# Six edits and three smaller ones at once in a tuned training step: later gradient transposes, the time reorder on VectorE, earlier down weights, k copied in parts, a shared layer norm, three blocks at once in the down product; more buffers for two tiles, a later pump

## The chip, the cores and the metric

One core of one Trainium2 chip. The metric is the device time of one execution in microseconds (us), the median of several executions. One execution is also profiled. Two of all executions were in a slower state (one of the kernel before in the first group of experiments, one of d2_act at 2229.60 us); the ratios leave them out, the medians do not; the granted clock of TensorE stands beside the profiled ones where it matters. Engines: PE is TensorE (matmul), DVE is VectorE, ACT is ScalarE, POOL is GpSimd, SP is SyncE, which in these kernels only issues transfers. `L938` is a line of the kernel file, and the line numbers move between versions.

## The reference, cut

The kernel computes the output and all gradients of this block in bf16, for 2048 positions, 1024 channels and 3584 hidden channels:

```python
xn = layernorm(q)
k_shift = sum_t pad(k)[t:] * shift_k[:, t]              # 4 taps
kv = k_shift * v
y  = long_convolution(kv, ssm_k) + kv * ssm_D           # by FFT in the reference, over 2048 positions
g  = silu((xn @ w_gate * (xn @ w_up)) @ w_down)
out = q + (xn * y) * g
# returned: out, and d/d(q, k, v, shift_k, ssm_k, ssm_D, w_gate, w_up, w_down) for grad_out
```

## The kernel before

PE works through five stages one after the other: gate and up product (`psg`), down product (`psbm`), backward through the down product (`psdh`) mixed with the weight gradients of gate and up (`psdw`), the weight gradient of down with the transposes of the weights (`wn`), and the gradient of the input (`psx`). The long convolution, forward and backward, is made of small matmuls (`psS`, `psP`, `psY`) with much DVE work between, and a "pump" slips it in between the large matmuls.

Work that needs an engine's result soon after is put off by a short list: `flush(n)` runs what has waited for n calls.

```python
def flush(age=0):
    for e in later: e[0] += 1
    while later and later[0][0] >= age: later.pop(0)[1]()

def dh_half(fc, hf, wdt, dgu):                       # backward through down, one hidden block
    gut = bg.tile([P, 2, 1024], BF16, name="gul", bufs=4)
    ld(gut[:], GUTd[fc, :, :, hf * 1024:(hf + 1) * 1024])            # ld: issued by SP
    for k in range(2):
        ...                                                            # 8 matmuls into psdh
        nc.scalar.copy(out=dht[:, k * 512:(k + 1) * 512], in_=ps[:])  # ACT frees the PSUM
        flush(2)
        btick(1)
    with tc.high_priority(60):
        tt(dgt[:], gut[:], dht[:]..., MUL)                             # DVE: "gul"
    def turn():
        sta(DGUTd[...], dgt[:]...)                                     # sta: issued by ACT
        for a in range(2):
            ...                                                        # PE: 8 transposes into tr
            nc.scalar.copy(out=dgu[:, :, a, ...], in_=ps[:])           # ACT: "U<-tr"
    defer(turn)

def dh_tail(ds, G, ew):                              # gradient of ssm_k, in time order
    ho = ew.tile([P, 2, P, 8], BF16, name="ho")
    for c in range(2):
        for rq in range(2):
            ...                                                        # 16 matmuls into psY
            nc.scalar.activation(ho[:, c].rearrange("p u r -> p r u")[:, 4 * rq:4 * rq + 4], ps[:], ACT.Copy, scale=WSC)
```

The down product takes its first two blocks of 128 positions together, so that each MB of weights (`WD`, held in the tiles U0 to U6) serves two, and loads `wdt`, the weights transposed by the transfer, only when it is over. [...]

## Time and profile before

| | before |
|---|---|
| median | 2256.11 us (2255.44 to 2267.16, 3 runs) |
| profiled span, clock | 2265.1 us, 0.984 |
| PE, DVE, ACT busy | 94%, 58%, 34% |

PE is the bound, so a part of the change counts as far as it shortens what PE waits. How much that can be is one subtraction. I took every matmul's start from the trace and compared the distance to the next start with the steady one, 0.216 us for 512 columns. What exceeds it is idle time, or, in stretches in which the granted clock was half, a doubled distance. The steady distances sum to 2082.1 us of the 2265.1; the rest, 183 us, is loss.

### The profile page before, as it was taken

The numbers are of one execution on the slowest core, as the hardware profiler recorded it, in microseconds if no ns is written. First come the engines' busy times: TensorE is split into PE (matmuls) and PEld (weight loads), VectorE is DVE, ScalarE is ACT, GpSimd is POOL, SyncE is SP. The second block draws the span as 40 slices with busy tenths as digits, with TensorE's granted clock in tenths as the row PEclk, the third lists the DMA queues.
The fourth block names the chain that finished last, engine by engine and source line by source line (L and its number), as shares of the span: only waits on it lengthen the run. The fifth ranks groups of instructions, "written<-read, shape, count | busy, mean of one in ns | idle before, by whom it ended". The sixth has DMA issues, their size and how long they took to land.

```text
span 2265.1 us, 29905 instructions
## 1 busy us (share of the span) xinstructions
PE 2122.9 (94%) x12128; PEld 1096.0 (48%) x12128; DVE 1311.4 (58%) x1770; ACT 769.3 (34%) x1040; POOL 273.8 (12%) x440
## 2 busy tenths in 40 slices
PE   5899999999899889989999999988998999999997
PEld 3455555555344455544545545444443455444443
DVE  8779898987354555659775676674456202222122
ACT  4433434343233343333333335554411242111111
POOL 3211111111021110011211200000021000000000
PEclk9999999999999999999999999999999999999999
DMA  9646565555977786686886755546688865323221
GB/s 312 232 175 231 190 207 196 189 174 188 323 233 231 246 263 198 167 258 200 251 211 209 226 163 168 177 160 188 138 240 146 235 216 173 135 107 117 103 107 33
DMA packets 386795, 436.92 MB, mean 193 GB/s; under 512 B 120960, under 2 KB 304280, under 8 KB 375520
## 3 DMA queue, kind: packets, MB, share of 16 engines
q1 hardware_dynamic: 227664, 177.23, 27.7%
q0 software_dynamic: 40944, 175.96, 22.5%
q10 hardware_dynamic: 118048, 81.81, 12.4%
q8 instruction: 95, 1.56, 0.3%
q14 instruction: 44, 0.36, 0.0%
HBM read 237.76 MB, written 179.34 MB: 184 GB/s over the span
## 4 chain that ended last, share of the span: by engine, by line
issue 27%; PE 21%; DVE 7%; ACT 4%; DMA 4%; POOL 1%; ACTq 1%; POOLq 0%; DVEq 0%
PE psdw L938 11%; PE psdw L1007 3%; DVE m L182 3%; PE psdh L915 3%; ACT ho L758 2%; ACT U L931 1%; PE tr L930 1%; DVE gul L182 1%; ACTq L67 1%; PE psY L755 1%; PE psY L314 1%; DMA DYFd<-DX 1%; DVE A L182 1%; POOL out_dram L64 1%; DVE W L182 1%
## 5 line engine op out<-in xcount | busy, mean ns | idle before, releaser
L463 PE MATMUL psg<-U,wslab 128*128 128x512 bf16 x1792 | 407.5, 383 | 9.2 <-ACT gut L465 5.6
L938 PE MATMUL psdw<-U,U 128*128 128x512 bf16 x1792 | 408.0, 382 | 1.3 <-ACT wb L942 1.3
L1063 PE MATMUL psx<-U,dgut 128*128 128x512 bf16 x1408 | 308.5, 379 | 0.0
L463 PEld LDWEIGHTS <-wslab 128*128 128x128 bf16 x1792 | 176.3, 99 | 208.4 <-issue 17.2
L1063 PEld LDWEIGHTS <-dgut 128*128 128x128 bf16 x1792 | 174.7, 98 | 208.1
L938 PEld LDWEIGHTS <-U 128*128 128x128 bf16 x1792 | 174.1, 99 | 193.9 <-issue 6.9
L465 ACT CAST gut<-psg 128x512 bf16<-128x512 f32 x224 | 130.9, 585 | 269.7 <-PE psg L463 252.0
L915 PE MATMUL psdh<-U,wdt 128*128 128x512 bf16 x896 | 213.4, 385 | 6.7 <-DMA wdt<-in_B_w_down_dram 6.7
L813 PE MATMUL psbm<-U,ht 128*128 128x512 bf16 x896 | 199.4, 383 | 10.0 <-DMA ht<-HTd 10.0
L1007 PE MATMUL psdw<-U,U 128*128 128x512 bf16 x896 | 201.6, 381 | 0.0
L182 DVE TENSOR_TENSOR m<-A,B 128x1024 bf16<-128x1024 bf16 (+1 forms) x160 | 116.7, 792 | 92.7 <-DMA B<-KFd 72.0
L942 ACT CAST wb<-psdw 128x512 bf16<-128x512 f32 x112 | 66.5, 594 | 249.8 <-PE psdw L938 213.3
L182 DVE TENSOR_TENSOR dxn<-psx,dxna_t 128x1024 f32<-128x1024 f32 x16 | 19.6, 1224 | 220.8 <-PE psx L1063 220.7
L813 PEld LDWEIGHTS <-ht 128*128 128x128 bf16 x896 | 87.8, 99 | 115.0 <-DMA ht<-HTd 11.0
L931 ACT COPY U<-tr 128x1024 bf16<-128x1024 bf16 x112 | 114.2, 1019 | 59.5 <-PE tr L930 38.0
L1007 PEld LDWEIGHTS <-U 128*128 128x128 bf16 x896 | 86.5, 98 | 98.4 <-issue 1.7
L915 PEld LDWEIGHTS <-wdt 128*128 128x128 bf16 x896 | 86.5, 99 | 95.7 <-DMA wdt<-in_B_w_down_dram 7.2
L182 DVE TENSOR_TENSOR W<-W,psP 128x512 f32<-128x512 f32 x128 | 81.6, 683 | 63.7 <-ACT W L214 54.0
L1079 ACT ACTIVATE junk<-dxn 128x1024 bf16<-128x1024 f32 x16 | 16.9, 1057 | 279.8 <-DVE dxn L182 279.8
L917 ACT CAST dht<-psdh 128x512 bf16<-128x512 f32 x112 | 68.8, 615 | 93.0 <-PE psdh L915 70.0
L182 DVE TENSOR_TENSOR gul<-gul,dht 128x2048 bf16<-128x2048 bf16 x56 | 68.4, 1221 | 53.4 <-ACT dht L917 48.1
L930 PE MATMUL tr<-ident,gul 128*128 128x128 bf16 x896 | 69.5, 221 | 26.6 <-ACT U L931 13.1
(220 smaller groups left out, 2520.5 us busy)
## 6 DMA issues: line engine op xcount, KB each, us to landing
gul<-GUTd SPq DMA_DIRECT2D x56, 512.0 KB, 5.9
DGUTd<-gul ACTq DMA_DIRECT2D x56, 512.0 KB, 5.9
dgut<-DGUTd SPq DMA_DIRECT2D x16, 1792.0 KB, 8.3
GUTd<-gut ACTq DMA_DIRECT2D x48, 512.0 KB, 3.9
A<-DYFd POOLq DMA_DIRECT2D x16, 1024.0 KB, 5.8
out_dram<-wb ACTq DMA_DIRECT2D x224, 64.0 KB, 2.4
ht<-HTd SPq DMA_DIRECT2D x7, 1792.0 KB, 8.3
HTd<-hT POOLq DMA_DIRECT2D x48, 256.0 KB, 3.4
```

The lines of the kernel that those rows point to most:

```text
L182: V.tensor_tensor(o, a, b, op)
L463: nc.tensor.matmul(ps[:], w[:, dc, a, fi * P:(fi + 1) * P], XNT[q][:, dc, :], start=(dc == 0), stop=(dc == DC - 1))
L465: nc.scalar.copy(out=gut[:, a, k * 512:(k + 1) * 512], in_=ps[:])
L813: nc.tensor.matmul(ps[:, dh * 512:(dh + 1) * 512], ht[:, fc, i * P:(i + 1) * P], WD[fc // 4][:, fc % 4, dh * 512:(dh + 1) * 512], start=(f ...
L915: nc.tensor.matmul(ps[:], wdt[:, dc, fi * P:(fi + 1) * P], DBMT[2 * hf + k][:, dc, :], start=(dc == 0), stop=(dc == DC - 1))
L917: nc.scalar.copy(out=dht[:, k * 512:(k + 1) * 512], in_=ps[:])
L930: nc.tensor.transpose(ps[:, i, :], dgt[:, a, i * P:(i + 1) * P], ident[:])
L931: nc.scalar.copy(out=dgu[:, :, a, fi * P:(fi + 1) * P], in_=ps[:])
L938: nc.tensor.matmul(ps[:].rearrange("p a f -> p (a f)"), XN[b // 4][:, b % 4, dc * P:(dc + 1) * P], dgus[b // 8][:, b % 8].rearrange("p a f ...
L942: nc.scalar.copy(out=wb[:], in_=ps[:])
L1007: nc.tensor.matmul(ps[:], h[:, b, fi * P:(fi + 1) * P], DBM[b // 4][:, b % 4, dh * 512:(dh + 1) * 512], start=(b == 0), stop=(b == NB - 1))
L1063: nc.tensor.matmul(ps[:, dh * 512:(dh + 1) * 512], t[a][:, 4 * j + f, i * P:(i + 1) * P], WGU[n][:, f, dh * 512:(dh + 1) * 512], start=(n ...
```

## The change

Its intent: take away PE's waits one by one. The diff, cut to its core:

```diff
@@ layer norm of blocks 0 to 3: subtraction on ACT; Wbc copies after it
-            V.tensor_scalar(x4[:, i, :], x4[:, i, :], mean_f[:, i:i + 1], None, op0=SUB)
+            eng.activation(x4[:, i, :], x4[:, i, :], ACT.Identity, bias=mean_n[:, i:i + 1])
[...]
@@ gate/up
-        gut = fg.tile([P, 2, 1024], BF16, name="gut")
+        gut = fg.tile([P, 2, 1024], BF16, name="gut", bufs=3)
@@ k copied to its padded place: 2 of 8 copies at the start, 2 each at hidden blocks 4, 8, 14
-    for ds in range(8):
-        ld(KSLd[ds, ...], kin[...])
+    copy_k(0)
+        if fc in (4, 8, 14):
+            copy_k({4: 1, 8: 2, 14: 3}[fc])
@@ time reorder
-                nc.scalar.activation(ho[:, c].rearrange("p u r -> p r u")[:, 4 * rq:4 * rq + 4], ps[:], ACT.Copy, scale=WSC)
-                yield 0.1
+                V.tensor_scalar(ho[:, c].rearrange("p u r -> p r u")[:, 4 * rq:4 * rq + 4], ps[:], WSC, None, op0=MUL)
+                yield 0.7
@@ gradient of k
-        acc = ew.tile([P, 2, 8, P], BF16, name="dka")
+        acc = ew.tile([P, 2, 8, P], BF16, name="dka", bufs=2)
-        ps = ps_y.tile([P, 4, P], F32, name="psY")
+        ps = ps_c3.tile([P, 4, P], F32, name=("psS", "psP")[ds % 2])
@@ down product
-    WD = [u8(j, a=4) for j in range(7)]
-    DBMT = [u8(7 + q, a=DC) for q in range(4)]
+    WD = [u8(j, a=4) for j in (10, 9, 8, 7, 4, 5, 6)]
+    DBMT = [u8(q, a=DC) for q in range(4)]
[...]
+    hts = [mh.tile([P, NF, 256], BF16, name="ht") for i in range(2)]
+    for q in range(2): load_ht_part(hts[0], 0, 14 * q, 14 * q + 14)
+    load_wd(0); load_wd(1)
+    for q in range(2): load_ht_part(hts[1], 1, 14 * q, 14 * q + 14); load_wd(2 + q)
+    for j in range(4, 7): load_wd(j)
-        for i in range(2): bm_mm(pss[i], ht, i, fc)
+        for b in range(3): bm_mm(pss[b], hts[b // 2], b % 2, fc)
+        if b == 10: wdt = load_wdt(0)
[...]
@@ backward: pump 8 ticks later, transposes later
-        bpump(bcnt[0] / BT)
+        bpump((bcnt[0] - 8) / (BT - 8))
-            flush(2)
+            flush(4)          # in dh_half
-            flush(2)
+            flush(3)          # in dw_slab
```

More of the change, by code (lines that the diff above doesn't have):

```diff
@@ L396, in ln_load, with layer_norm @@
         return x4
-    def layer_norm(b0, n, x4):
+    def layer_norm(b0, n, x4, eng):
         def small(name, dt=F32):
@@ L410, in layer_norm @@
         V.tensor_copy(mean_f, mean_b)
+        if eng is not None:
+            mean_n = small("mean_n")
+            V.tensor_scalar(mean_n, mean_b, -1.0, None, op0=MUL)
         var_b = small("var_b", BF16)
@@ L432, in layer_norm @@
             q, qi = divmod(b, 4)
-            V.tensor_scalar(x4[:, i, :], x4[:, i, :], mean_f[:, i:i + 1], None, op0=SUB)
-            V.tensor_scalar(x4[:, i, :], x4[:, i, :], RSTD[:, b:b + 1], None, op0=MUL)
+            if eng is None:
+                V.tensor_scalar(x4[:, i, :], x4[:, i, :], mean_f[:, i:i + 1], None, op0=SUB)
+            else:
+                eng.activation(x4[:, i, :], x4[:, i, :], ACT.Identity, bias=mean_n[:, i:i + 1])
+            last = V.tensor_scalar(x4[:, i, :], x4[:, i, :], RSTD[:, b:b + 1], None, op0=MUL)
             ps = ps_st.tile([P, DC, P], BF16, name="tr")
@@ L439, in layer_norm @@
         st(XNd[:, b0:b0 + n, :], x4[:, 0:n, :])
+        return last
     later = []
@@ L575, in build_kernel, with copy_k @@
     slabs.append(load_slab(1, nc.sync))
-    for ds in range(8):
-        ld(KSLd[ds, 3:3 + S, :].rearrange("(p a) d -> p a d", a=16),
-           kin[:, ds * P:(ds + 1) * P].rearrange("(p a) d -> p a d", a=16))
+    def copy_k(dp):
+        for ds in (2 * dp, 2 * dp + 1):
+            tc.keep_in_program_order(
+                ld(KSLd[ds, 3:3 + S, :].rearrange("(p a) d -> p a d", a=16),
+                   kin[:, ds * P:(ds + 1) * P].rearrange("(p a) d -> p a d", a=16)))
+    copy_k(0)
     for c in xs[:2]:
-        layer_norm(*c)
+        last = layer_norm(*c, nc.scalar)
     for q in range(4):
         if q > 0:
-            layer_norm(*xs[q + 1])
+            layer_norm(*xs[q + 1], None)
         for fc in range(4):
@@ L586, in build_kernel @@
         if q == 0:
-            build_bcast()
+            with tc.issue_after(last.ins):
+                build_bcast()
         if q == 1:
@@ L620, in build_kernel @@
     U += [ub.tile([P, 4096], BF16, name=f"U{i}") for i in range(4, 11)]
+    bw = pool("bw", 2, side="right")
     mh = pool("mh", 2, side="right")
@@ L799, in dk_unit @@
         yield 1.5
-    C_TOTAL = 8 * (FWD4_W + 0.8) + 16 * (PROD_W + INV_W) + 8 * 1.4 + 8 * 5.4 + 8 * 0.5 + 8 * 11.2
+    C_TOTAL = 8 * (FWD4_W + 0.8) + 16 * (PROD_W + INV_W) + 8 * 1.4 + 8 * 5.4 + 8 * 2.9 + 8 * 11.2
     bpump, bdrain = make_pump(conv_backward(), C_TOTAL)
     ddo = const.tile([P, 8], BF16, name="ddo")
-    WD = [u8(j, a=4) for j in range(7)]
+    WD = [u8(j, a=4) for j in (10, 9, 8, 7, 4, 5, 6)]
     def load_wd(j):
         ld(WD[j], B_w_down[j * 512:(j + 1) * 512, :].rearrange("(c p) d -> p c d", p=P))
-    DBMT = [u8(7 + q, a=DC) for q in range(4)]
+    DBMT = [u8(q, a=DC) for q in range(4)]
     def bm_mm(ps, ht, i, fc):
@@ L857, in load_ht, with load_wdt, load_ht_part @@
         return ht
-    ht = mh.tile([P, NF, 256], BF16, name="ht")
-    for j in range(7):
-        if j % 2 == 0:
-            f0, f1 = 4 * j, min(4 * j + 8, NF)
-            ld(ht[:, f0:f1], HTd[f0 * P:f1 * P, 0:256].rearrange("(c f) s -> f c s", f=P))
+    def load_wdt(sl):
+        wdt = bw.tile([P, DC, SLW], BF16, name="wdt")
+        nc.sync.dma_start_transpose(out=wdt[:], in_=B_w_down[sl * SLW:(sl + 1) * SLW, :])
+        return wdt
+    def load_ht_part(ht, bp, f0, f1):
+        ld(ht[:, f0:f1], HTd[f0 * P:f1 * P, bp * 256:(bp + 1) * 256].rearrange("(c f) s -> f c s", f=P))
+    hts = [mh.tile([P, NF, 256], BF16, name="ht") for i in range(2)]
+    for q in range(2):
+        load_ht_part(hts[0], 0, 14 * q, 14 * q + 14)
+    load_wd(0)
+    load_wd(1)
+    for q in range(2):
+        load_ht_part(hts[1], 1, 14 * q, 14 * q + 14)
+        load_wd(2 + q)
+    for j in range(4, 7):
         load_wd(j)
-    pss = [ps_bm.tile([P, D], F32, name="psbm") for i in range(2)]
+    pss = [ps_bm.tile([P, D], F32, name="psbm") for i in range(3)]
     for fc in range(NF):
-        for i in range(2):
-            bm_mm(pss[i], ht, i, fc)
-    for i in range(2):
-        gate(i, pss[i])
-    for bp in range(1, 8):
-        ht = load_ht(bp)
-        for i in range(2):
-            ps = ps_bm.tile([P, D], F32, name="psbm")
-            for fc in range(NF):
-                bm_mm(ps, ht, i, fc)
-                if fc == 14:
-                    flush()
-            gate(2 * bp + i, ps)
+        for b in range(3):
+            bm_mm(pss[b], hts[b // 2], b % 2, fc)
+    for b in range(3):
+        gate(b, pss[b])
+    ht = hts[1]
+    for b in range(3, NB):
+        bp, i = divmod(b, 2)
+        if i == 0:
+            ht = load_ht(bp)
+        if b == 10:
+            wdt = load_wdt(0)
+        ps = ps_bm.tile([P, D], F32, name="psbm")
+        for fc in range(NF):
+            bm_mm(ps, ht, i, fc)
+            if fc == 14:
+                flush()
+        gate(b, ps)
     for p_ in (ps_tr, ps_bm, mo, mt, mi, mh):
         p_.release()
-    XN = [u8(q, a=4) for q in range(4)]
-    bw = pool("bw", 2, side="right")
+    XN = [u8(7 + q, a=4) for q in range(4)]
     bg = pool("bg", 2, side="right")
@@ L898, in btick @@
         bcnt[0] += n
-        bpump(bcnt[0] / BT)
-    def load_wdt(sl):
-        wdt = bw.tile([P, DC, SLW], BF16, name="wdt")
-        nc.sync.dma_start_transpose(out=wdt[:], in_=B_w_down[sl * SLW:(sl + 1) * SLW, :])
-        return wdt
+        bpump((bcnt[0] - 8) / (BT - 8))
     def dh_half(fc, hf, wdt, dgu):
@@ L952, in load_h @@
         return h
-    wdt = load_wdt(0)
     flush()
@@ L962, in build_kernel @@
     first = dh_slab_half(0, 0, wdt)
-    DBM = [u8(7 + q, a=4) for q in range(4)]
+    DBM = [u8(q, a=4) for q in range(4)]
     for sl in range(NSL):
@@ L1022, in build_kernel @@
     gd = pool("gd", 1)
-    stores = [u8(i, a=4) for i in range(4)] + [gw.tile([P, 4, D], BF16, name=f"W{i}")[:] for i in range(3)]
+    stores = [u8(7 + i, a=4) for i in range(4)] + [gw.tile([P, 4, D], BF16, name=f"W{i}")[:] for i in range(3)]
     def early():
@@ L1097, in build_kernel @@
         if n >= 7:
-            run(build_wgu(n, u8(n - 3, a=4), gn, ps_tr))
+            run(build_wgu(n, u8((4, 5, 6, 0, 1, 2, 3)[n - 7], a=4), gn, ps_tr))
         for i in range(2):
```

## The prediction

> **What bounds the kernel now.** I read the page first. Its busy line:
>
> ```profile
> PE 2122.9 (94%) x12128; PEld 1096.0 (48%) x12128; DVE 1311.4 (58%) x1770; ACT 769.3 (34%) x1040; POOL 273.8 (12%) x440
> ```
>
> TensorE (PE) is busy for 94% of a profiled span of 2265.1 us and nothing else is above 58%, so PE sets the end. The changed kernel, as built, issues the same 12128 matmuls, so only PE's idle time, and the clock it loses after idling, can be won. The second view, PE's waits by releaser (total us, times, longest), says which:
>
> ```profile
> PE tr L437 <- DVE x L434: 20.6, 3, 16.1
> PE psY L755 <- ACT ho L758: 19.8, 11, 5.8
> PE tr L930 <- ACT U L931: 13.1, 11, 3.7
> PE tr L930 <- DVE gul L182: 11.6, 5, 4.6
> PE psbm L813 <- DMA ht<-HTd: 10.0, 2, 5.5
> PE psY L314 <- DVE HX L182: 7.1, 7, 1.3
> PE psdh L915 <- DMA wdt<-in_B_w_down_dram: 6.7, 1, 6.7
> PE psY L791 <- DVE dt L182: 6.7, 2, 6.2
> PE tr L997 <- DMA wn<-in_B_w_up_dram: 6.6, 3, 4.8
> PE psg L463 <- ACT gut L465: 5.6, 2, 5.1
> PE psY L646 <- DMA dyx<-DYd: 3.7, 1, 3.7
> ```
>
> These eleven rows are 111.5 us. Each part of the change aims at one of them, except HX, most of the first row (16.1 us before the first transpose) and wn. Third, PE's timeline (start, length, then the idle time before it in brackets), where the down product starts, ends, and where a gradient transpose is late:
>
> ```profile
> 573.63 25.86 PE L813 MATMUL psbm<-U,ht 128*128 128x512 bf16 x112 [5.47 <-DMA ht<-HTd]
> 604.00 6.17 PE L813 MATMUL psbm<-U,ht 128*128 128x512 bf16 x20 [4.52 <-DMA ht<-HTd]
> ...
> 793.63 1.46 PE L915 MATMUL psdh<-U,wdt 128*128 128x512 bf16 x3 [6.74 <-DMA wdt<-in_B_w_down_dram]
> ...
> 999.95 1.03 PE L930 MATMUL tr<-ident,gul 128*128 128x128 bf16 x8 [3.16 <-DVE gul L182]
> 1000.78 2.75 PE L915 MATMUL psdh<-U,wdt 128*128 128x512 bf16 x6
> ```
>
> The last row shows a second cost: 6 matmuls in 2.75 us is double the usual spacing of 0.216 us. By start-to-start spacing I find 14 such stretches of 3.4 or 6.8 us after 27 us, 61 us together (ten of 3.4, four of 6.8), each in or behind an idle stretch: about 31 us lost beyond the idle. The total of idle is 142 us (2265.1 less 2122.9).
>
> **What the Trainium skill says.**
> 1. "TensorE: Matmul & The Clock Gate", Part 1: the PE clock is halved after an idle window of about 3.4 us and stays so for a window of 3413 ns. This trace agrees in length (3.4 and 6.8 us), but here gaps of 3.2 us were enough, as above. So a gap of 3 to 7 us costs 1.7 or 3.4 us more.
> 2. "SBUF — State Buffer", Door 1, the note on cachelines: writes that cross to a new 16-byte line each time pay a penalty. The eviction ho on ACT writes bf16 with a step of 8 elements, exactly 16 bytes. The trace agrees with a penalty on ACT: ho took 2456 ns, the plain eviction of the same 512 columns, gut, 585 ns. No VectorE (DVE) instruction in this trace writes with that step, so whether DVE pays is unknown.
> 3. "DMA: Bandwidth & Descriptors", Issuing engines are not separate DMA queues: all share the 16 engines. The trace agrees: the wdt transpose waited 6.7 us behind 4 MB of other loads.
>
> **The change part by part.**
>
> *Layer norm, k copy, third gut buffer (0 to 110 us).* Four subtractions of 0.476 us leave DVE for ACT (1.9 us), and four copies of Wbc (0.750 us each, 3.0 us) move behind the first scaling. But in the built order DVE does more statistics before the first scaling (663 ns each), and PE has eight transposes of hrow before the first gate/up matmul, whose load is issued only at about 19 us. I put the first gate/up matmul at 26 to 27 us instead of 24.3: 2 to 3 lost. Later blocks are earlier by about 1 to 3 us. The third gut buffer lets ACT evict while GUTd stores are slow: its 5.1 us gap and its clock window (1.7) mostly go. Three of four pairs of k copies leave the crowded start; two land at about 94 us, in other crowded traffic. Net: 4 saved.
>
> *Down product (560 to 810 us).* Three blocks at once make 24 matmuls (24 x 0.216 = 5.2 us) out of each MB of weights instead of 16 (3.5 us), and both ht tiles come first in halves; so the 4.5 us gap and its clock window (1.7) go. wdt is now loaded during the product, so 6.7 and 3.4 (6.8 us at half) go; the backward pump starts 8 ticks later, so 3.7 and 1.7 of dyx go. That is 21.7. Against it: the first matmul needs the first weights in U10, which were being read until the last gate/up matmul (567.9 us) and now stand in the queue behind about 2.7 MB of others, wdt among them; at the 316 GB/s that the window 560 to 600 shows, about 3.7 MB take 11 us. The gap grows from 5.5 to 9 to 11, and the cold window may become 6.8 us. Loss 6. Net: 16.
>
> *Gradient transposes (810 to 1650 us).* They now wait for four (in the other loop three) later groups instead of two, 3.5 to 7 us of PE work. The gaps before them were 0.7 to 4.7 us. The two rows tr are 24.7 us; with the windows at 1000, 1055 and 1181 us (13.6 us at half, so 6.8) 31.5. I take 80%: 25.
>
> *Time order by DVE (1360 to 1641 us).* ACT loses 32 x 2.456 = 78.6 us; DVE gains 32 x 0.69 = 22 us if a strided write costs it no more than its 512-column PSUM operation (683 ns). DVE is 58% busy, ACT free to do the U copies. The row is 19.8 us, plus a window of 6.8 at 1549 (3.4), 23.2. But DVE executes in order and has waited 72.0 us for B<-KFd, up to 23.9 at once; ho then waits behind that. I take 75%: 17.
>
> *Gradient of k (1650 to 1800 us).* DVE stood 10.2 us behind the store of dka, so dt was 6.2 us late and PE ran half speed for 6.8. Two buffers for dka, and alternate PSUM tiles, take away 6.2 + 3.4 less a rest: 8. The load of dkh (2.7) stays. wn at 1797 us (4.8 + 1.7) stays, as the order of that queue is the same.
>
> Sum: 4 + 16 + 25 + 17 + 8 = 70 us. New small waits usually appear where several waits are removed at once; I take off 10%, as a choice, not a measurement: 63. From the median 2256: **2193 us**, 2.8% faster.
>
> **The rivals.**
> *DVE becomes the place of wait.* If the strided write costs DVE what it costs ACT (2.456 us), DVE gains 79 us instead of 22, in 280 us in which its windows already show up to 29.9 busy of 40. For: the same step of 16 bytes, and the skill's note. Against: neither names DVE, and the pacing number beside the instruction in the diff goes from 0.1 to 0.7, which reads as DVE time. Then the ho waits stay as DVE waits, and late gul come on top: about 2215. I give it one in four.
> *The waits move.* The transposes may be late enough, but the product psdw needs what they make, and the four gul buffers come free later, so gul loads start later. For: DVE already waited 5.0 us for gul<-GUTd. Against: psdw waited only 1.3 us. With half of the 25 lost: about 2205.
> *The transfer at the head of the down product.* The order of the queue could make the first down matmul wait 14 us or more, and the start could be later by 5: about 2202.
> *Everything goes.* If all targeted rows and windows go and the start is not later: of about 173 us lost now (142 idle, 31 clock), the targeted terms above come to 4 + 22 + 31 + 23 + 10 = 90, and small ones beside them to a few: about 2160.
>
> **Range and chances.** Two rivals together give 2225, the best case 2160, so 8 in 10 lie in 2163 to 2222. Faster by 2% means under 2211, which needs 45 of the 70 us; the first rival alone does not quite allow it. Faster 0.80, within 2% 0.19, slower 0.01, as nothing is added to PE and only the head of the down product and the start have a known loss.
>
> **What the profile of after would show.** PE still about 2100 to 2120 us busy in a span of about 2200; ho on DVE at about 0.7 us (2.4: the first rival); no row psY from ACT ho, and one from DVE ho under 6 us; the rows tr from gul and U together under 6 us; one gap before the first psbm of 9 to 11 us and none at the second group of weights; psdh at the product's end without its 6.7; the dt row under 1 us; wn unchanged at about 5. The prediction is wrong if a new row above 10 us stands in PE's waits, if the first psg is later than 30 us, or if the half-clock windows do not fall from 14 to about 5.

## The result

| | before | changed |
|---|---|---|
| median | 2256.07 us (4 runs) | 2313.38 us (2310.04 to 2316.85, 4 runs) |
| ratio to before | | 1.0242, 95% interval 1.0207 to 1.0278 |
| profiled span, clock | 2265.1 us, 0.984 | 2310.0 us, 0.976 |

It is 2.4% slower, where I had 2.8% faster. A ratio here is the mean time of one kernel's fast runs over that of the other's fast runs of the same rounds, so it is not quite the ratio of the medians. Executions over 1.5% slower than the fastest of the same kernel are left out of the means. One per cent is 22.6 us.

The busy line of the changed kernel's page, then PE's waits by releaser (total us, times, longest):

```profile
PE 2128.7 (92%) x12128; PEld 1098.6 (48%) x12128; DVE 1384.8 (60%) x1798; ACT 695.0 (30%) x1010; POOL 276.4 (12%) x440
```

```profile
PE psY L770 <- DVE ho L773: 32.8, 13, 6.9
PE tr L443 <- DVE x L440: 26.1, 3, 18.0
PE psbm L828 <- DMA U<-in_B_w_down_dram: 16.5, 1, 16.5
PE tr L1022 <- DMA wn<-in_B_w_up_dram: 12.3, 3, 10.1
PE psS L806 <- DMA dkh<-DKSHd: 11.7, 4, 7.3
PE tr L865 <- DVE dbm L182: 11.5, 14, 6.9
PE tr L956 <- ACT U L957: 10.0, 8, 6.9
PE psP L201 <- DVE W L182: 8.3, 3, 7.8
PE psY L314 <- DVE HX L182: 7.1, 7, 1.3
PE psdh L941 <- ACT dht L943: 6.8, 3, 3.4
PE psS L201 <- ACT W L214: 6.5, 1, 6.5
```

The old rows that the change aimed at are indeed gone or smaller: no row from gul, none from ht, wdt, dyx or dt, and gut is down to 0.5. New ones stand in their place and are larger in sum. The stretches at half clock grew too, by the trace's clock records between 27 us and the last matmul: from 14, 61 us together, to 16, 102 us together. DVE's busy time rose by 73 us where I had reckoned 22. The groups of instructions, one line for ho of each kernel (busy us, mean ns, then the idle time before it), first before, then changed:

```profile
L758 ACT ACTIVATE ho<-psY 128x512 bf16<-128x512 f32 x32 | 78.6, 2456 | 28.6 <-PE psY L755 20.5 <-DMA out_dram<-ho 4.0 <-issue 2.7
```

```profile
L773 DVE TENSOR_SCALAR ho<-psY 128x512 bf16<-128x512 f32 x32 | 77.8, 2431 | 47.0 <-PE psY L770 44.5 <-DMA out_dram<-ho 2.5
```

DVE took 2431 ns for what took ACT 2456. Three more places, from PE's timeline of the changed kernel (start, length, and in brackets the idle before):

```profile
135.90 1.04 PE L201 MATMUL psP<-kv,TF 128*128 128x256 bf16 x4 [7.78 <-DVE W L182]
...
593.40 6.89 PE L828 MATMUL psbm<-U,ht 128*128 128x512 bf16 x22 [16.51 <-DMA U<-in_B_w_down_dram]
...
673.18 1.04 PE L865 MATMUL tr<-ident,dbm 128*128 128x128 bf16 x8 [6.93 <-DVE dbm L182]
```

The first follows from DVE standing still for k, as DVE's timeline shows just before:

```profile
124.79 1.23 DVE L182 TENSOR_TENSOR acc<-k,Wbc 128x2048 bf16<-128x2048 bf16 x1 [14.22 <-DMA k<-KSLd]
```

That load was issued only after two of the postponed copies of k (issued from 100.6 us, landed at 114.4 and 118.1), because it reads what they write. The second is the head of the down product: the first ht was issued at 576.4 us, as soon as a store of the forward convolution (YFd) had landed, for which SP had stood, and the first weights only at 581.7, behind three pieces of ht of 0.9 MB; they landed at 593.3. The third: three gates now want DVE at once, and the inputs of the fifth came late; its first operation stood until the load of yf_t landed at 667.3, and the transposes of its dbm were due at 666 (some expectations below call this the third gate).

The loss by stage, in us of PE time beyond the steady distance (idle plus what half clock cost), from the profiled run of each kernel. The third stage ends here with the last psdh, and the fourth holds all after it. The last two columns are experiments told below: both mends in the changed kernel (the order in which ho is written, and the queue of one store's trigger: after_rs), and the best version found (d2_again). Each column is one execution: two profiles of the same kernel (d2 and d2_again) differ by up to 6 us in a stage.

| stage, to its last matmul | before | changed | after_rs | d2_again |
|---|---|---|---|---|
| start, gate/up | 53.4 | 62.1 | 64.4 | 49.6 |
| down product | 18.7 | 32.9 | 32.9 | 13.9 |
| backward through down, gate/up gradients | 69.8 | 75.9 | 41.0 | 39.8 |
| down gradient, weight transposes | 41.1 | 56.9 | 13.7 | 17.1 |
| sum | 183.0 | 227.8 | 152.0 | 120.4 |
| span less the sum | 2082.1 | 2082.2 | 2082.3 | 2082.3 |

The last row is the same by construction, since all four issue the same matmuls and each loss is a distance less the steady one; it checks the sums alone. Every stage lost.

### The profile page after: what moved, and what is told of

It is laid out like the page before. It is cut to its first block, busy times and chain, and to the rows that moved or that the text cites. A ratio compares the mean times of both kernels' runs of the same rounds, so it can differ in the third digit from the quotient of the medians.

```text
span 2310.0 us, 29873 instructions
## 1 busy us (share of the span) xinstructions
PE 2128.7 (92%) x12128; PEld 1098.6 (48%) x12128; DVE 1384.8 (60%) x1798; ACT 695.0 (30%) x1010; POOL 276.4 (12%) x440
## 3 DMA queue, kind: packets, MB, share of 16 engines
q10 hardware_dynamic: 118048, 81.81, 11.7%
## 4 chain that ended last, share of the span: by engine, by line
issue 42%; PE 23%; DVE 19%; DMA 8%; POOL 4%; ACT 2%; ACTq 0%; SPq 0%; POOLq 0%; DVEq 0%
PE psdw L964 9%; DVE m L182 5%; PE psg L470 4%; DVE W L182 3%; PE psdh L941 3%; DVE HX L182 2%; PE psbm L828 2%; PE psY L314 1%; DMA B<-KFd 1%; DVE ho L773 1%; ACT U L957 1%; POOL out_dram L64 1%; DVE A L182 1%; PE tr L956 1%; DVE gul L182 1%
## 5 line engine op out<-in xcount | busy, mean ns | idle before, releaser
L964 PE MATMUL psdw<-U,U 128*128 128x512 bf16 x1792 | 415.5, 382 | 2.6 <-ACT U L957 2.6
L941 PE MATMUL psdh<-U,wdt 128*128 128x512 bf16 x896 | 208.3, 383 | 8.1 <-ACT dht L943 6.8
L828 PE MATMUL psbm<-U,ht 128*128 128x512 bf16 x896 | 199.1, 383 | 16.7 <-DMA U<-in_B_w_down_dram 16.5
L1032 PE MATMUL psdw<-U,U 128*128 128x512 bf16 x896 | 202.9, 382 | 0.0
L968 ACT CAST wb<-psdw 128x512 bf16<-128x512 f32 x112 | 65.7, 586 | 284.9 <-PE psdw L964 270.6
L773 DVE TENSOR_SCALAR ho<-psY 128x512 bf16<-128x512 f32 x32 | 77.8, 2431 | 47.0 <-PE psY L770 44.5
L1035 ACT CAST wb<-psdw 128x512 bf16<-128x512 f32 x56 | 32.8, 587 | 204.6 <-PE psdw L1032 195.4
```

Of the source, the lines that this page charges most:

```text
L773: V.tensor_scalar(ho[:, c].rearrange("p u r -> p r u")[:, 4 * rq:4 * rq + 4], ps[:], WSC, None, op0=MUL)
L828: nc.tensor.matmul(ps[:, dh * 512:(dh + 1) * 512], ht[:, fc, i * P:(i + 1) * P], WD[fc // 4][:, fc % 4, dh * 512:(dh + 1) * 512], start=(f ...
L941: nc.tensor.matmul(ps[:], wdt[:, dc, fi * P:(fi + 1) * P], DBMT[2 * hf + k][:, dc, :], start=(dc == 0), stop=(dc == DC - 1))
L964: nc.tensor.matmul(ps[:].rearrange("p a f -> p (a f)"), XN[b // 4][:, b % 4, dc * P:(dc + 1) * P], dgus[b // 8][:, b % 8].rearrange("p a f ...
L968: nc.scalar.copy(out=wb[:], in_=ps[:])
L1032: nc.tensor.matmul(ps[:], h[:, b, fi * P:(fi + 1) * P], DBM[b // 4][:, b % 4, dh * 512:(dh + 1) * 512], start=(b == 0), stop=(b == NB - 1))
```

## The experiments

Eighteen runs. Kernels of one group ran on one chip and shared its runs of the kernel before (medians 2261, 2260, 2260 and 2261 us; groups 3 and 4 shared theirs), so I compare their ratios to before. All results were correct. "Changed" is 1.0242.

### Group 1: one thing undone or mended in the changed kernel

**u_ho**: ho back on ACT, with its old weights in the pacing of the pump (not shown).

```diff
-                V.tensor_scalar(ho[:, c].rearrange("p u r -> p r u")[:, 4 * rq:4 * rq + 4], ps[:], WSC, None, op0=MUL)
+                nc.scalar.activation(ho[:, c].rearrange("p u r -> p r u")[:, 4 * rq:4 * rq + 4], ps[:], ACT.Copy, scale=WSC)
```

> The changed kernel with the time reorder (ho) back on ACT and its old weights in the pacing; all else as changed. Theory A (ho on DVE is the largest loss: 2431 ns each instead of the 690 ns I had counted, 78 us of DVE in 280 us, so that DVE is late with everything behind it): PE's wait for ho falls from 32.8 to about 20 or less, the waits for W and dkh that came after it shrink, and the time falls by 25 to 40 us, to about 2280. Theory B (the loss is at the head, in the k copies and the down product, and ho is as bad on either engine): under 12 us, to about 2305.

Measured 2266.17 us, ratio 1.0031 (0.9971 to 1.0090): 2.1 points, some 48 us, less than changed, more than theory A had said. PE's wait for ho fell to 19.5. So the move of ho is the largest single loss.

**r_in**: ho stays on DVE, with the four time rows innermost.

```diff
-                V.tensor_scalar(ho[:, c].rearrange("p u r -> p r u")[:, 4 * rq:4 * rq + 4], ps[:], WSC, None, op0=MUL)
+                V.tensor_scalar(ho[:, c, :, 4 * rq:4 * rq + 4], ps[:].rearrange("p i u -> p u i"), WSC, None, op0=MUL)
```

> The changed kernel, ho still on DVE, but the four time rows innermost: it writes 4 neighbouring bf16 (8 bytes) before each step to the next 16 bytes, and reads PSUM with a step of 512 bytes instead. The result is the same. If the step of 16 bytes at every single element on the write side costs the 1.75 us: ho takes 0.7 to 1.2 us and the time falls by 25 to 40 us as with ho on ACT, or more. If the reading side with a step costs as much: ho stays at 2.4 us or over and the time is unchanged.

Measured 2265.75 us, ratio 1.0023 (0.9977 to 1.0069). Its group of ho:

```profile
L773 DVE TENSOR_SCALAR ho<-psY 128x512 bf16<-128x512 f32 x32 | 22.0, 689 | 62.0 <-PE psY L770 60.6 <-DMA out_dram<-ho 1.4
```

689 ns, the 690 that I had put into the sum, from the same values in another order. The cost was the order of the writes: one bf16 in every 16 bytes against four neighbours. Reading PSUM with a step of 512 bytes cost nothing that shows (683 ns for a plain operation of that size). The time falls by 49 us, as with ho on ACT.

But now ho costs what I predicted and the kernel still takes 2266, not 2193. So the mis-sized ho is not the whole error.

**u_k**: the eight copies of k at the start, as before.

> The changed kernel with all eight copies of k at the start, as before. Theory: the two copies at 100 us hold back the loads of k behind them, DVE idles 14.2 us there, PE 7.8 us and half clock after it. Without it: DVE's wait for k from KSLd falls from 14 to about 5 us, PE's wait for W near 128 us goes, the time falls by 8 to 12 us, to about 2303. Rival (the wait comes from the wslab loads that were there anyway): no change, or the start loses 2 to 5 us.

Measured 2301.18 us, ratio 1.0189 (1.0140 to 1.0238): 12 us by the means, but the interval overlaps that of changed. The wait of 7.8 us was gone; one for gate/up weights (4.0) came in its place.

**u_down**: the down product as before.

> The changed kernel with the down product as before (two blocks, first weights in U0, wdt loaded at its end). Theory: the change gained 4.7 + 1.7 (second ht) and 6.9 + 3.4 (wdt) and lost 11 at its head, 7 at the third gate (665 us) and 3 to 5 of clock: undone, the time moves by under 5 us either way. Rival (the new order of the loads costs more than it hides): falls by 8 us or more.

Measured 2293.51 us, ratio 1.0136 (1.0090 to 1.0182): 24 us less than changed: the rival (8 us or more) came true. The change of the down product was a loss. The wait for the first matmul fell back to 5.8 us, and those for the second ht (3.7) and wdt (7.2) returned.

### Group 2: where the later transposes went

In r_in the two rows of gradient transposes had fallen from 24.7 to 9.7 us, as predicted, yet the third stage lost 59.7 us there against 69.8 before, and the 10 us are those of wdt at its start: nothing that shows of the 25 for the transposes, nor of the 17 for ho, had arrived. New rows had come: psdh on the eviction dht, psdw on U. So this group starts from **m1**, the changed kernel with ho as in r_in, the k copies and the down product as before.

> The changed kernel less its three known losses: ho on DVE with the time rows innermost (691 ns), the k copies all at the start and the down product as before. What stays of the change: layer norm, third gut buffer, later transposes, two dka buffers, the pump 8 ticks later. If the losses add up (47 for ho, 12 for k, 24 for the down product, from the runs before): about 2313 - 83 = 2230, 1% faster than before. If they overlap (a later start of the backward part hides behind the same waits): about 2250.

Measured 2259.67 us, ratio 0.9973 (0.9935 to 1.0011). The three losses did not add up: 12 + 24 us undone gave 11 together over r_in, and the intervals of the two overlap. The second alternative was nearer.

**m1_noflush**: m1 with the transposes at their old place (`flush(2)` twice).

> As m1, with the gradient transposes at their old place. Theory (the deferral only moves the wait from the transposes to the evictions of dht and to psdw, 10 + 15 us instead of 25): the same time as m1 within 8 us. What I predicted blind (25 us gained by it): 20 us or more slower than m1.

Measured 2243.20 us, ratio 0.9931 (0.9880 to 0.9981): faster by the means, though the intervals overlap. The deferral for which I had counted 25 us gained nothing. m1's profiled run shows why, at its worst. Its PE, DVE and ACT in the same stretch (timelines; ACTq is ACT's sequencer, which issues transfers):

```profile
1080.51 1.86 PE L923 MATMUL psdh<-U,wdt 128*128 128x512 bf16 x4 [21.29 <-ACT dht L925]
```

```profile
1051.09 1.22 DVE L182 TENSOR_TENSOR gul<-gul,dht 128x2048 bf16<-128x2048 bf16 x1
1076.86 1.22 DVE L182 TENSOR_TENSOR m<-A,B 128x2048 bf16<-128x2048 bf16 x1 [24.55 <-issue]
1078.00 1.22 DVE L182 TENSOR_TENSOR gul<-gul,dht 128x2048 bf16<-128x2048 bf16 x1
```

```profile
1052.99 1.07 ACT L925 CAST dht<-psdh 128x512 bf16<-128x512 f32 x2 [6.93 <-DVE gul L182]
1079.25 0.59 ACTq L67 DMA_DIRECT2D DGUTd<-gul  x1
1079.88 0.58 ACT L925 CAST dht<-psdh 128x512 bf16<-128x512 f32 x1 [25.81 <-DVE gul L182]
```

Read it from the bottom of the chain. A load of A was issued at 1048.06 and landed at 1076.78. The convolution's product with A came before the second gul in DVE's queue and held it back until 1078.00, though the inputs of that gul (its load landed by 1027, its dht was written by 1054.1) had been ready for 24 us. ACT's queue has the trigger of the store of that gul to DGUTd; it waited there. The eviction of dht, which needs nothing from gul, stood behind the trigger. PE ran out of PSUM. So moving the transposes later on PE moved nothing for ACT: the path from DVE to PE ran through a trigger in ACT's queue. (The "issue" beside DVE's 24.55 us means that the profile shows no releaser; that it was the load is my reading of its landing time.) The 28.7 us of that load are an extreme: it shared the 16 engines with a transposing transfer of wdt that took 29.9 us, against 4 to 18 us in the kernel before.

**m1_late**: the trigger after the transposes and copies of the same deferred step.

```diff
     def turn():
-        sta(DGUTd[...], dgt[:]...)
         for a in range(2): ...
+        sta(DGUTd[...], dgt[:]...)
```

> As m1, but in each deferred step the store of gul to DGUTd comes after the transposes and copies in the program, so its trigger stands later in ACT's queue. Theory (ACT waits in its queue for gul from DVE at this trigger, and dht evictions, which free PE's PSUM, wait behind it): PE's waits for dht and for psdw on U shrink from about 12 to under 6 us, 5 to 10 us faster than m1. Rival (ACT would stop at the copies of U all the same): no change.

Measured 2248.75 us, ratio 0.9948 (0.9910 to 0.9986): inconclusive against m1. PE's wait for dht fell from 28.8 to 9.7, but that for U rose from 4.8 to 13.4: ACT now stood at the copies.

**m1_spq**: the trigger in SP's queue.

```diff
-        sta(DGUTd[...], dgt[:]...)
+        ld(DGUTd[...], dgt[:]...)        # issued by SP
```

> As m1, with that trigger in SP's queue instead of ACT's. Same theory: ACT no longer waits for gul at a trigger at all, PE's waits for dht go, 5 to 15 us faster than m1. Rival (SP now stands there, and the loads of gul and wdt behind it come late): PE's waits for gul or wdt grow, and it is slower than m1.

Measured 2219.76 us, ratio 0.9815 (0.9784 to 0.9845): 36 us faster than m1 with one word changed. ACT's wait, by releaser, first in m1, then in m1_spq:

```profile
ACT dht L925 <- DVE gul L182: 47.7, 7, 25.8
```

```profile
ACT dht L925 <- DVE gul L182: 9.3, 3, 5.1
```

The row of PE's waits for dht is gone. SP now waits 170.9 us for gul, which costs little, as SP only issues transfers. What is not separated: the loads behind the trigger in SP's queue, wdt among them, are now issued later too, and that may have helped; the longest transfer of wdt fell from 29.9 us to 15.4. That m1 met one slow transfer is not the whole of it: in r_in the longest took 18.3 us, and there the same edit still gave 28 us (after_rs, below).

### Group 3: do the mends hold in the changed kernel?

**after_rs**: the whole change, with the edits of r_in and m1_spq.

> The whole changed kernel with two mends of one line each: ho with the time rows innermost, and the trigger of the store to DGUTd on SP's queue instead of ACT's. If the two mends add up to what they gave apart (2.2% and 1.6%): ratio to before about 0.985, 2225 us. If my blind sum holds apart from these two mis-sized terms: 2193 plus the losses of the head (k copies 10, first down matmul 11, third gate 7 + clock), also about 2225. If the mends hide behind the same waits: about 2250.

Measured 2238.02 us, ratio 0.9897 (0.9837 to 0.9957): 1.3 points, 28 us, under r_in, by the trigger alone. It is 1% faster than before. The table of stages shows where both mends together act: the third stage lost 41.0 us in place of 75.9 and the fourth 13.7 in place of 56.9, while the first two still lost what they had.

**m1_spq_noflush**: m1_spq with the transposes at their old place.

> The fastest so far (m1 with the trigger on SP), with the gradient transposes at their old place. Theory (deferral is worth its 25 us only when ACT does not stand at the trigger): 12 to 25 us slower than with it, PE's waits of the transposes for gul and U back at 15 or more. Rival (the trigger was all, the deferral is worth nothing): the same within 6 us.

Measured 2239.41 us, ratio 0.9894 (0.9843 to 0.9944); m1_spq was 0.9815 in the group before, and the next kernel, m1_spq but for the layer norm, 0.9789 in this one. So the deferral is worth some 18 to 24 us when ACT doesn't stand at the trigger, near the 25 of the prediction; the intervals only just touch. PE's transposes waited 14.3 us for gul here, and 1.4 in m1_spq. The two edits need each other: with the transposes at their old place the new trigger gives 8 us (0.9931 to 0.9894, not clear), with the later transposes 36.

**m1_spq_noln**: m1_spq with the layer norm as before.

> The fastest so far with the layer norm as before (subtraction on DVE, Wbc in the middle). The trace of the changed kernel has the first gate/up matmul 2 to 3 us later: without this part, 2 to 5 us faster. Rival (the later blocks of the layer norm gain that back): the same.

Measured 2214.73 us, ratio 0.9789 (0.9735 to 0.9842). Not clear against m1_spq.

**d1**: the new down product back in, with the k copies at the start and both mends. The loads of the head are in the order of use, the first ones in pieces of 4 hidden blocks (ht) and 2 (weights), and the transposes of a gate come one block later, with a third buffer for dbm (not shown).

```diff
+    part(0, 0, 4); wdp(0, 0, 2); part(1, 0, 4); wdp(0, 2, 4)
+    part(0, 4, 14); wdp(1); part(1, 4, 14); wdp(2); wdp(3)
+    part(0, 14, 28); part(1, 14, 28); wdp(4); wdp(5); wdp(6)
[...]
-                flush()
+                flush(2)
```

> The fastest so far with the new down product put back in, mended: the first loads in the order of use and in small pieces, and each gate's transposes one block later. The gap before the first down matmul falls from 16.7 to about 7, the one of 7 at the third gate goes, those of the second ht (3.7) and wdt (6.7) stay gone: 10 to 15 us faster than the fastest so far, about 2207. Rival (the pieces make the loads slower, PE waits again in the first 20 us): the same or slower.

Measured 2214.93 us, ratio 0.9794 (0.9744 to 0.9844). The waits at the fifth gate (the third in the expectation), the second ht and wdt were gone, but the head was a miss. PE's timeline of d1:

```profile
584.97 15.39 PE L822 MATMUL psbm<-U,ht 128*128 128x512 bf16 x57 [12.84 <-DMA U<-in_B_w_down_dram]
```

The trace of the transfers names the culprit: the scheduler had put eight loads for the gates (2 MB, issued from 572.2 to 577.6 us) ahead of the first weights, which were issued at 578.1.

### Group 4: the head once more, and the rest

45 us were still unexplained: after_rs took 2238 where the prediction had 2193.

**d2**: as d1, with the gate loads queued behind all weights, and the layer norm as before.

```diff
-    for b in range(3): gate(b, pss[b])
+    with tc.issue_after(last_wd.ins):
+        for b in range(3): gate(b, pss[b])
```

> The changed kernel with both mends (ho with rows innermost, trigger on SP), the k copies and the layer norm as before, and the down product mended once more: the loads of the first three gates, 2 MB, now stand behind all weights (in d1 eight of them went ahead of the first weights). The gap before the first down matmul falls from 13.0 (d1) to 5 to 7 us, the clock windows there shrink: 2196 to 2206 us, ratio 0.973 to 0.977. If another transfer takes their place: as d1, 0.979.

Measured 2211.95 us, ratio 0.9765 (0.9704 to 0.9826). The head is mended. PE's timeline of d2:

```profile
571.39 1.86 PE L814 MATMUL psbm<-U,ht 128*128 128x512 bf16 x4 [4.58 <-DMA U<-in_B_w_down_dram]
```

The time is not clear against d1. Nor is it against m1_spq_noln (0.9789), from which d2 differs by the down product alone: 3 to 5 us for d2 and d2_again. So the mended down product no longer costs time, but that it gains the predicted 16 us is not shown.

**d2_k** and **d2_ln**: d2 with the k copies in parts, and d2 with the shared layer norm.

> As d2 with the k copies in parts, as in the change. Theory (the copies at about 100 us hold back the loads of k for DVE's next group): PE waits 8 us near 128 us and runs 3.4 to 6.8 us at half clock, 8 to 12 us slower than d2. Rival (what they hold back is hidden, as the backward part catches up): the same within 3 us.

> As d2 with the layer norm shared with ACT, as in the change. Theory (more statistics ahead of the first scaling, hrow's transposes ahead of the first gate/up matmul): PE starts 2 to 3 us later and idles more up to 90 us, 3 to 7 us slower than d2. Rival: the same within 2 us.

Measured 2215.82 us (0.9780, 0.9719 to 0.9842) and 2212.49 us (0.9778, 0.9727 to 0.9828). Neither is clear against d2. In d2_k PE's idle stretch of 8.2 us near 120 us was there again, but its profiled span was only 6 us longer than d2's. In d2_ln PE's wait for the first transpose was 17.9 us against 16.0, but its span was 1 us shorter than d2's. So neither part made the 45 us. The head of the down product is what is left, together with its fifth gate: by subtraction, some 30 us from after_rs (0.9897) to d2 (0.9765).

**b_sfr**: the kernel before with only three edits: `flush(4)` and `flush(3)`, ho on DVE as in r_in, and the trigger on SP.

> The kernel before with only three small edits: the transposes later, the trigger on SP, ho on DVE with rows innermost. By the sums of the runs: 20 us for the deferral with a free ACT, 7 for the trigger alone, and some 5 to 10 for ho: 2222 us, ratio 0.983 to 0.987. If the mends only work together with the dka buffers and the later pump: 0.99 or more.

Measured 2237.17 us, ratio 0.9890 (0.9841 to 0.9940). That is 15 us short of the sum that was expected. m1_spq_noln (0.9789) has the same three edits and besides them the third gut buffer, the two dka buffers with alternate PSUM tiles, and the later pump: 23 us less, with intervals that only just touch. So these make the rest, though none of them was run alone. PE waited 7.2 us for gut, 5.1 for dt and 3.4 for dyx in b_sfr, and for none of them in m1_spq_noln; by the distances between matmuls, some 19 us of the difference lie in the fourth stage, where dka is.

### Group 5: was DVE needed at all?

**d2_act**: d2 with ho on ACT, rows innermost, and its old weights in the pacing (not shown). **d2_again**: d2, in five rounds.

```diff
-                V.tensor_scalar(ho[:, c, :, 4 * rq:4 * rq + 4], ps[:].rearrange("p i u -> p u i"), WSC, None, op0=MUL)
+                nc.scalar.activation(ho[:, c, :, 4 * rq:4 * rq + 4], ps[:].rearrange("p i u -> p u i"), ACT.Copy, scale=WSC)
```

> As d2, but ho is evicted by ACT again, with the four time rows innermost in its write, as DVE has it in d2. If the step of 16 bytes alone made ho slow on ACT too: about 0.6 us each instead of 2.456, PE's wait for ho falls from 10.6 to under 6 us, DVE is 22 us freer, and it is as fast as d2 or up to 8 us faster: then moving ho to DVE was never needed. If ACT reads PSUM slowly with a step of 512 bytes: ho stays above 1.5 us and it is 5 to 15 us slower than d2.

> The same kernel as d2, in five rounds, to narrow the interval: 2203 to 2214 us, ratio 0.974 to 0.980.

d2_act took 2213.19 us (2196.58 to 2229.60, ratio 0.9771, 0.9732 to 0.9809), d2_again 2209.10 us (ratio 0.9771, 0.9746 to 0.9795). The group of ho in d2_act:

```profile
L759 ACT ACTIVATE ho<-psY 128x512 bf16<-128x512 f32 x32 | 19.2, 599 | 19.7 <-PE psY L756 17.8 <-issue 1.8
```

599 ns in place of 2456, with the engine unchanged. PE has no row of waits for ho at all in d2_act. ho never had to leave ACT. (The kernel before with this edit alone was not run.) The time is that of d2, so the two are equal choices here. d2_again beats both kernels: 2.3% less than before. Its busy line and PE's largest waits:

```profile
PE 2112.1 (96%) x12128; PEld 1092.5 (50%) x12128; DVE 1330.9 (60%) x1802; ACT 694.7 (32%) x1008; POOL 273.5 (12%) x440
```

```profile
PE tr L437 <- DVE x L434: 20.6, 3, 16.3
PE psY L756 <- DVE ho L759: 11.4, 9, 3.7
PE tr L1021 <- DMA wn<-in_B_w_up_dram: 7.3, 3, 5.4
```

The start, 16.3 us before the first transpose, is now the largest loss, and no edit here touched it with success.

## Why the prediction was wrong

By its own steps:

- **What bounds the kernel** held: PE's matmuls are the same and the time moved with what PE lost (183 us before, 228 changed, 120 in d2_again). Two readings under it were loose. The 3.2 us taken as enough for half clock is no threshold: in the kernel before a gap of 3.67 us (at 964.2) was followed by none, and in d2_again one of 2.05 us (at 953.7) by 3.4 us of it. And wdt did not stand 6.7 us behind other loads: it was issued only at 786.92, as PE went idle, and took 6.66 us, with two of the four 1 MB loads before it still under way.
- **Time order by DVE, "32 x 0.69 = 22 us if a strided write costs it no more"**: this is the step that failed, and the largest. Measured 2431 ns, 77.8 us. I had the rival and the page for it, gave it one chance in four and 22 us (2215 instead of 2193). It came, and cost 48 to 49 us (u_ho, r_in). The mechanism was named rightly and mis-sized by half: I added the late ho alone, and not that everything else in DVE's queue in that stage comes late too.
- **Gradient transposes, "I take 80%: 25"**: the sum was right and its ground was not. The rows did fall, from 24.7 to 10.0 us, and the deferral is worth 18 to 24 us, but only once the trigger of DGUTd is off ACT's queue. With it there, m1 was no faster than m1_noflush. My rival "the waits move" looked at psdw and at gul's loads, and left out that ACT, which frees the PSUM of psdh, waits for gul itself. That is worth 28 us of the changed kernel (r_in against after_rs).
- **Down product, "Net: 16"**: wrong in sign; undone, it gave 24 us. The gains were there (no wait for the second ht, wdt or dyx). The gap at the head was 16.5 us and not 9 to 11, my third rival's "14 us or more". The wait at the fifth gate (6.9) was in none of my steps. Both can be mended (d2), but the mended product stands only 3 to 5 us, not clear of noise, under the old one (m1_spq_noln).
- **Layer norm, k copies, third gut buffer, "Net: 4 saved"**: the first stage lost 62.1 us instead of 53.4. The gut wait went from 5.6 to 0.5. The first gate/up matmul began at 28.6 us, not 26 to 27. The k copies cost a wait of 7.8 us that I didn't see, though I had noted that two of them land in crowded traffic: I asked whether they slow others, and not who reads what they write. In the whole time neither part is clear (d2_k, d2_ln).
- **Gradient of k, "8"**: the wait for dt went. In the changed kernel dkh took its place (11.7); that row is not among the larger ones once ho and the trigger are mended. The part alone was not tested; with the gut buffer and the pump it is worth some 23 us (b_sfr against m1_spq_noln).
- **The range** failed as a sum. I let two rivals together make 2225. All three came at once and each was larger than I had said. With ho, the trigger and the head mended, and the k copies and layer norm left as before, the parts give 2209, 16 us above the prediction: most of the intent was sound, and details of its making cost about 100 us. That 2209 comes near 2193 does not confirm the sum part by part: it stands without two of the parts, and with a down product that is not shown to give its 16. Of the signs of being wrong that the prediction named, two came: new rows above 10 us (32.8 for ho the largest) and more half-clock stretches.

What stays open: how much of the gain of m1_spq comes from the later issue of wdt in SP's queue; why the trigger itself sometimes took 3 to 7 us in ACT's queue; and what the gut and dka buffers and the pump give alone.

## What to carry to other kernels

Before an operation is moved to another engine because it is slow there, change the order in which it writes: here the same values cost 599 or 2456 ns on one engine and 689 or 2431 on the other. When PE's work is put off to get past a late engine, follow every queue between that engine and PE, transfer triggers included; here a trigger that waited for data stopped ACT's evictions behind it for up to 25.8 us. And when several waits are removed at once, measure each part with the others mended: single gains of 12 and 24 us gave 11 together, and one of about 20 showed only after a word was changed elsewhere.

## What the Trainium skill lacked or had wrong

- "SBUF — State Buffer", Door 1, the note on cachelines: it says that each access that crosses to a new 16-byte line pays, and gives no size, and of engines GpSimd's probes alone. The runs give them for writes: with one bf16 per 16 bytes 2431 ns on DVE and 2456 on ACT for 512 columns (4.8 ns each), with four neighbours 689 and 599, so both engines pay alike. No run had a step between, so that the line is the cause is not shown. It gives no cost of a step for DVE or ACT reading PSUM; with fp32 and a step of 512 bytes the runs show none to speak of (689 against 683 ns, 599 against 585).
- "TensorE: Matmul & The Clock Gate", Back-to-back issue gap: it gives about 131 ns for each matmul of 512 columns in a sustained stream. Here such streams ran at 216 ns throughout, which is what it gives for an isolated one, and what Part 1 of the same page gives back to back (215.7 ns).
- "DMA: Bandwidth & Descriptors", Issuing engines are not separate DMA queues: it says that issuing from several engines saves only the small time of the trigger. Here the choice of the issuing engine for one store went with 28 us (r_in to after_rs) and 36 us (m1 to m1_spq) of 2260. A trigger that waited for data held back ACT's computing behind it, 25.8 us at the worst; how much of the gain is the later issue of the loads behind it in SP's queue is not separated.
